# Second MoE on one Trainium2 core: fourteen layer-one products in a run, then the layer-two products of the quad before

## The chip, the cores and the metric

The kernel runs on one core of a Trainium2 chip. The metric is the device time of one execution in microseconds (us), taken as the median of several executions. PE is the matrix engine, DVE, ACT and POOL are the vector, scalar and GpSimd engines, and SP is the engine whose queue issues the transfers here.

## The reference, cut to what matters

The program computes an attention, a dense two-layer network, and a second mixture of experts. Only the last part is touched. It is dense: every expert sees every token.

```python
for e in range(8):                      # N = 2304 tokens, D = 512, F = 1024
    h = np.maximum(x @ w1[e], 0.0)      # layer one: 2304x512 @ 512x1024
    ye = h @ w2[e]                      # layer two: 2304x1024 @ 1024x512
    out += P[:, e:e + 1] * ye           # P: Sinkhorn-balanced gate, 2304x8
```

## The kernel before, in words

Every float32 product is made of three matmuls on rounded halves of the operands (`mm3`, lines 126 to 128: high by high, high by low, low by high). In the second MoE each layer's block product is done by seven products instead of eight (a Strassen-like scheme with sums t1 to t4 of the blocks). A *product* of either layer is six matmuls of 384 columns.

The tokens lie in three blocks of 768. Block one is handled by an earlier stage (layer one from the tile `w1a`, layer two with 512 columns in `values`). Blocks two and three are handled in *quads*: quad m covers 512 columns of one expert's hidden layer, that is two pairs of seven layer-one products, so fourteen; m runs from 16 to 47, sixteen quads a block. Quads 31 and 47, the last of each block, use plain products in layer two (`PLAIN`).

`step(m, s)`, s from 0 to 13, sets the order by hand, for all engines (instructions are issued in the order of the code). A step has one layer-one product s of quad m (`g_product`: weights `w1o`, moving operand `xb..` or `xt..`) and one layer-two product s of quad m-1 (`y_product`: weights `w2o`, moving operand `rb..` or `rt..`). So PE alternates: six matmuls of layer one, six of layer two, and so on.

Layer one of a pair: its seven products (0 to 6, in the order of `GP`) go to three PSUM banks. Products 0, 2, 4 and 5 accumulate in v1 one after the other, product 1 goes to v3, 3 and 6 to v2. After products 0, 2 and 4 ACT must copy v1 out (to m1, u2 and u3) before the next product may add to it. `g_evict` joins the parts: after product 1 DVE adds v3 to m1, after product 4 v2 to u3, after product 6 v2 to u2, each into the temporary, and ACT rectifies the sum (line 1575) into the hidden tile R[m, f, h] (f, h: which 256-column half, which 384-token half). After product 5 ACT rectifies v1 itself. m1 and u3 share one buffer, u2 has its own.

Then R is weighted by the gate (`scaled`, line 1449, DVE), the sums t1 to t4 are made in place (`r_sum`, lines 1454 to 1460, DVE), and each of the seven operands is split: ACT rounds it (`r_hi`, line 1468), POOL takes the rest (`r_lo`, line 1473). Layer two accumulates in four PSUM banks; after each product DVE adds the bank to the output accumulator (line 1509).

SP issues the weights: `load_w1` (line 791) eight layer-one products ahead in a ring of eight buffers, `w2_op` (line 1485) one tile of 512 KB every second step in a ring of nine.

The tiles lie in pools on two sides of SBUF: `w2o` and the operands `rb..`, `rt..` in one pool on the left, `xb..`, `xt..` and `w1o` in two neighbouring pools on the right. In the earlier stage `w1a` lies in the right pool for even pairs n and in the left one for odd n (`split_w1`).

Of the kernel before, what the change touches and what calls it, by code (L numbers as in the profile page):

```python
# [7 lines left out]

F32 = mybir.dt.float32
F32R = mybir.dt.float32r  # L10
U32 = mybir.dt.uint32
AF = mybir.ActivationFunctionType
# [6 lines left out]

F64_SMALL = 2.0 ** -15  # L20
F64_LARGE = 122879.984375


def raw(ap):
# [5 lines left out]
def attention_moe_moe2(  # L30
# [12 lines left out]
    nc = tc.nc  # L43
    P = 128
# [21 lines left out]
    HALF = 3 * P  # L66
    NB = NT // (2 * HALF)
    NPF = F2 // (2 * P)
    NP = E * NPF
# [601 lines left out]
    def gate_logits():  # L671
# [35 lines left out]
        ("t4", 3, 0, False, (1, 0)),  # L707
    ]

    YP_LAST = [  # L710
        ("b11", 0, 0, True),
        ("b21", 2, 0, False, (0, 0)),
# [70 lines left out]

    w1q = {}

    def load_w1(j):

        n, p = divmod(j, 7)
        if NP <= n < NB * NP and j not in w1q:
            w = w1q[j] = p3.tile([P, 2, 2, P], F32R, name="w1o", tag="w1o", bufs=8)  # L790
            nc.sync.dma_start(raw(w), d_w1[n % NP][:, GP[p][0]])

# [367 lines left out]
    def new_temp(nm, tag):  # L1160
        temps[nm] = p2.tile([P, HALF], F32, name=nm, tag=tag, bufs=1)
        return temps[nm]
# [226 lines left out]
    for n in range(NP):  # L1389
        if n == 0:  # L1390

            g_product(0, 0)
            nc.scalar.copy(new_temp("m1", "m"), gb[0][:, :HALF])
            g_product(0, 1)
            nc.vector.tensor_add(temps["m1"], gb[1][:, :HALF], temps["m1"])
            gate_sums(NCH - 1)
            g_product(0, 2)
            nc.scalar.copy(new_temp("u2", "u"), gb[0][:, :HALF])
            gate_logits()
            m1.close()  # L1400
            pp = ctx.enter_context(tc.tile_pool(name="pp", bufs=1))
            wps = ExitStack()
            wp = wps.enter_context(tc.tile_pool(name="wpa", bufs=1))
            acc = [wp.tile([P, 2 * HALF // P, DM], F32, name=f"o{e}") for e in range(2)]
            w2r[0] = raw_w2(0)
            hidden[0] = [wp.tile([P, 2, 2 * HALF], F32R, name=f"r{i}", tag=f"r{i}", bufs=2) for i in "hl"]
            rh, rl = [x[:, 0, :HALF] for x in hidden[0]]
            nc.scalar.activation(rh, temps["m1"], AF.Relu)
            nc.vector.scalar_tensor_tensor(rl, temps["m1"], 0.0, raw(rh), op0=ALU.max, op1=ALU.subtract)
            raw_w1(2)  # L1410
            w2r[1] = raw_w2(1)
            sums_w1(1, False)
        elif n == NP - 2:
            place = acc[1].rearrange("p t d -> p (t d)").rearrange("p (k c) -> p k c", c=HALF)
            x_load(NQ - 1, place, [p2.tile([P, 2, HALF], F32, name="xt", tag="Ra", bufs=4) for _ in range(2)])
        elif n == NP - 1:
            p3s.close()
            p3 = ctx.enter_context(tc.tile_pool(name="p3b", bufs=1, side="right"))
            for j in range(8):
                load_w1(7 * NP + j)  # L1420
        for p in range(3 if n == 0 else 0, 7):
            first_step(n, p)
        before = (n, hidden.pop(n), w2s[n])
        slab.pop(n)
# [20 lines left out]
    def scaled(m, f, h):  # L1445

        pb = pbs[m // NQ, m % NQ // PER][:, h * HALF : (h + 1) * HALF]
        r = R[m, f, h]
        nc.vector.tensor_mul(r, r, pb[:, None, :].to_broadcast([P, 2, HALF]))  # L1449

    def r_sum(m, nm):
        r = {(f, h): R[m, f, h] for f in range(2) for h in range(2)}
        if nm == "t1":
            nc.vector.tensor_sub(r[0, 0], r[0, 1], r[0, 0])  # L1454
        elif nm == "t2":
            nc.vector.tensor_sub(r[0, 0], r[1, 1], r[0, 0])
        elif nm == "t3":
            nc.vector.tensor_sub(r[0, 1], r[1, 1], r[0, 1])
        elif nm == "t4":
            nc.vector.tensor_sub(r[1, 0], r[1, 0], r[0, 0])  # L1460
# [14 lines left out]
    def r_op(m, nm):  # L1475
        r_hi(m, nm)
        if (m, nm) != (total - 1, "b21"):
            r_lo(m, nm, nc.gpsimd)

    def w2_op(m, i):  # L1480
        if m in PLAIN and i > 3:
            return
        o = (0, 2, 1, 3)[i] if m in PLAIN else YP[i][1]
        w = w2q[m, o] = wp.tile([P, 2, 2, 2 * P], F32R, name="w2o", tag="w2o", bufs=9)
        nc.sync.dma_start(raw(w), d_w2[m % NQ][:, o])

    def y_product(m, s):

        i, dt = divmod(s, 2)
        b, op, bk, first, *dsts = (YP_LAST if m in PLAIN else YP)[i]  # L1490
        if m < total - 1:
            bk %= 2
        ps = yb[2 * bk + dt]
        w, x = w2q[m, op], rop[m, b]
        ws = slice(dt * P, (dt + 1) * P)
        for a in range(2):
            mm3(
                ps[:, :HALF], (w[:, a, 0, ws], w[:, a, 1, ws]), (x[:, 0, a], x[:, 1, a]), first and a == 0, a == 1,
                skip_group_check=True,
            )  # L1500
        for dst in dsts:
            key = (m, dst, dt)
            if m % NQ == 0 and key not in touched:
                touched.add(key)
                if dt == 0:
                    acc[dst] = wp.tile([P, 2, HALF], F32, name=f"a{dst[0]}{dst[1]}", tag=f"a{dst[0]}{dst[1]}", bufs=1)
                nc.scalar.copy(acc[dst][:, dt], ps[:, :HALF])
            else:
                nc.vector.tensor_add(acc[dst][:, dt], ps[:, :HALF], acc[dst][:, dt])  # L1509
# [34 lines left out]
    def last_quad():  # L1544
# [16 lines left out]
        for second in range(2):  # L1561
            turn_out(NB - 1, (1, 1), second, yb[second], True)

    def step(m, s):

        nonlocal wp
        if m < total:
            pair, p = divmod(s, 7)

            def rectify(src, f, h):  # L1570
                if pair == 0:
                    R[m, f, h] = (p3 if m % 2 else p2).tile(
                        [P, 2, HALF], F32, name=f"R{f}{h}", tag="Rb" if m % 2 else "Ra", bufs=4
                    )
                nc.scalar.activation(R[m, f, h][:, pair], src, AF.Relu)  # L1575

            g_product(2 * m + pair, p)
            load_w1(7 * (2 * m + pair) + p + 8)
        old = NQ <= m - 1 < total
        if s in EARLY_OPS and m < total:  # L1580
            scaled(m, *EARLY_OPS[s][1:])
        elif s in LATE_OPS and old and m < total:
            if s == 0:
                scaled(m - 1, 0, 1)
            if m - 1 not in PLAIN:
                r_sum(m - 1, LATE_OPS[s])
        if m < total:
            g_evict(p, rectify)
        if s in EARLY_OPS and m < total:
            r_op(m, EARLY_OPS[s][0])  # L1590
        elif s in LATE_SPLITS and old and m < total:
            if m - 1 not in PLAIN:
                r_op(m - 1, LATE_SPLITS[s])
            elif s == 2:
                r_op(m - 1, "t3")
        if old:
            if m - 1 not in PLAIN:
                y_product(m - 1, s)
            else:
                for x in (s,) if s < 12 else (2 * s - 12, 2 * s - 11):  # L1600
                    y_product(m - 1, x)
        if m < total:
            x_switch(m, s)
            if m > NQ:
                if s % 2:
                    w2_op(m, s // 2)
            elif s < 6:
                values(before, (s,))
            elif s == 6:
                wps.close()  # L1610
                wp = ctx.enter_context(tc.tile_pool(name="wpb", bufs=1))
            elif s % 2:
                for i in range(4) if s == 7 else (s // 2,):
                    w2_op(m, i)
            if s == 4 and m % PER == PER - 1 and m + 1 < total:
                load_pb((m + 1) // NQ, (m + 1) % NQ // PER)
        for d in range(2):
            blk, q = divmod(m - d, NQ)
            if q == 0 and blk > 1:
                for dst, at in WHOLE:  # L1620
                    for x in range(2):
                        if at + x == s + 14 * d:
                            turn_out(blk - 1, dst, x, yb[x] if dst == (1, 0) else None)

    load_pb(1, 0)
    store_w2(NP - 1, w2s[NP - 1])
    for m in range(NQ, total):
        for s in range(STEPS):
            if s == 0 and (m + 1) % NQ == 0 and m + 1 < total:
                place = wp.tile([P, 8, HALF], F32, name="q")  # L1630
                x_load(m, place, [wp.tile([P, 2, HALF], F32, name=f"xt{i}") for i in range(2)])
            if (m, s) == (NQ, 7):
                acc = {}
                yb = [y_bank(f"y{i}") for i in range(4)]
            step(m, s)
# [29 lines left out]
```

## Time and profile before

| | us |
|---|---|
| median of 3 runs | 2055.83 (2054.61 to 2056.07) |
| the profiled execution | 2057.16, span 2055.4 |
| PE busy | 2017.4, 98% |
| DVE busy | 1440.3, 70% |
| POOL busy | 1069.4, 52% |
| ACT busy | 986.0, 48% |

The profile is that of one execution. The span runs from its first to its last instruction. A PE row's length is a latency: matmuls overlap, so the spacing of starts tells the rate, not the length.

### The profile page before, as it was taken

To read this page: it belongs to the slowest core of one execution; us is meant where nothing else is said; L and a number is where in the kernel's file an instruction comes from. 1 tells how busy PE (TensorE), PEld (TensorE's weight loads), DVE (VectorE), ACT (ScalarE), POOL (GpSimd) and SP (SyncE) were. 2 spreads that over 40 slices of the span, in tenths; PEclk is the share of its full clock that TensorE was granted. 3 is DMA by queue.
4 is the path that set the end of the run, shared out by engine and by line. 5 is a ranking of instruction groups with operands and counts; after the bars stand their busy time and mean duration, and the time that the engine had idled before them with its cause. 6 is when DMAs were issued, how large, how long until landed. Compare 5 with 4: busy or idle time off the path is not lost.

```text
span 2055.4 us, 31706 instructions
## 1 busy us (share of the span) xinstructions
PE 2017.4 (98%) x10821; PEld 1843.2 (90%) x10821; DVE 1440.3 (70%) x2572; ACT 986.0 (48%) x2006; POOL 1069.4 (52%) x821
## 2 busy tenths in 40 slices
PE   7989999999999999999999999999999999999999
PEld 5767777777888899999989999999999999999998
DVE  7987776565457877777785766776676577667765
ACT  7666665454354454444444434443444444444443
POOL 4224344431168788887884444554455454445442
PEclk9999999999999999999999999999999999999999
DMA  7877777337658878878889778787786877777883
GB/s 203 285 205 243 223 232 203 121 135 262 218 191 327 305 298 324 321 288 308 317 298 336 266 264 257 254 256 260 258 276 213 269 259 258 256 255 240 268 260 103
DMA packets 296416, 519.68 MB, mean 253 GB/s; under 512 B 91056, under 2 KB 137792, under 8 KB 292160
## 3 DMA queue, kind: packets, MB, share of 16 engines
q1 hardware_dynamic: 296256, 517.65, 75.1%
q8 instruction: 87, 1.43, 0.3%
q14 instruction: 73, 0.60, 0.1%
HBM read 356.53 MB, written 161.03 MB: 252 GB/s over the span
## 4 chain that ended last, share of the span: by engine, by line
PE 83%; DVE 6%; ACT 2%; DMA 2%; issue 1%; POOL 1%; SPq 0%; ACTq 0%; DVEq 0%; POOLq 0%
PE y L127 11%; PE y L126 11%; PE y L128 11%; PE g L126 11%; PE g L127 10%; PE g L128 10%; PE s L126 2%; PE s L128 2%; PE s L127 2%; PE acc L127 2%; PE acc L128 2%; PE acc L126 2%; PE h L126 1%; PE h L128 1%; PE h L127 1%
## 5 line engine op out<-in xcount | busy, mean ns | idle before, releaser
L1473 POOL TENSOR_TENSOR rb<-R,rb 128x768 fp32r<-128x768 f32 x95 | 213.9, 2252 | 345.7 <-ACT rb L1468 321.9
L1509 DVE TENSOR_TENSOR a<-y,a 128x384 f32<-128x384 f32 x420 | 232.7, 554 | 192.4 <-PE y L128 192.4
L1473 POOL TENSOR_TENSOR rt<-R,rt 128x768 fp32r<-128x768 f32 x121 | 230.2, 1915 | 138.8 <-ACT rt L1468 59.5
L118 POOL TENSOR_TENSOR w2a<-r,w2a 128x1024 fp32r<-128x1024 f32 x64 | 153.8, 2403 | 67.6 <-ACT w2a L117 67.6
L126 PE MATMUL g<-xt,w1o 128*128 128x384 f32 x512 | 173.7, 339 | 1.8 <-ACT u L1187 1.0
L128 PE MATMUL g<-xt,w1o 128*128 128x384 f32 x512 | 172.6, 337 | 0.0
L127 PE MATMUL g<-xt,w1o 128*128 128x384 f32 x512 | 172.3, 337 | 0.0
L126 PE MATMUL y<-rt,w2o 128*128 128x384 f32 x496 | 168.1, 339 | 0.0
L127 PE MATMUL y<-rt,w2o 128*128 128x384 f32 x496 | 167.9, 339 | 0.0
L128 PE MATMUL y<-rt,w2o 128*128 128x384 f32 x496 | 167.4, 337 | 0.0
L1468 ACT ACTIVATE rt<-R 128x768 fp32r<-128x768 f32 x122 | 102.7, 842 | 134.7 <-DVE R L1454 84.0
L128 PE MATMUL y<-w2a,rl 128*128 128x512 f32 x384 | 150.1, 391 | 0.0
L127 PE MATMUL y<-w2a,rh 128*128 128x512 f32 x384 | 149.6, 390 | 0.2 <-POOL w2a L118 0.2
L126 PE MATMUL y<-w2a,rh 128*128 128x512 f32 x384 | 149.4, 389 | 0.0
L1449 DVE TENSOR_TENSOR R<-R,pb 128x768 f32<-128x768 f32 x128 | 138.5, 1083 | 5.4 <-ACT R L1575 3.9
L126 PE MATMUL y<-rb,w2o 128*128 128x384 f32 x408 | 138.3, 339 | 0.6 <-DVE a L1509 0.6
L127 PE MATMUL y<-rb,w2o 128*128 128x384 f32 x408 | 138.2, 339 | 0.0
L128 PE MATMUL y<-rb,w2o 128*128 128x384 f32 x408 | 137.6, 337 | 0.0
L126 PE MATMUL g<-xb,w1o 128*128 128x384 f32 x384 | 129.9, 338 | 0.0
L128 PE MATMUL g<-xb,w1o 128*128 128x384 f32 x384 | 129.5, 337 | 0.0
L127 PE MATMUL g<-xb,w1o 128*128 128x384 f32 x384 | 129.3, 337 | 0.0
L1575 ACT ACTIVATE R<-u 128x384 f32<-128x384 f32 x128 | 67.3, 526 | 127.6 <-DVE u L1195 86.4
(331 smaller groups left out, 5847.2 us busy)
## 6 DMA issues: line engine op xcount, KB each, us to landing
w1o<-d_w SPq DMA_DIRECT2D x448, 256.0 KB, 3.1
w2o<-d_w SPq DMA_DIRECT2D x218, 512.0 KB, 4.0
d_w<-w1a SPq DMA_DIRECT2D x32, 1792.0 KB, 11.7
d_w<-w2a SPq DMA_DIRECT2D x30, 1536.0 KB, 7.8
r<-in_moe_w_dram SPq DMA_DIRECT2D x64, 512.0 KB, 4.2
u<-in_moe_w_in_dram SPq DMA_DIRECT2D x16, 512.0 KB, 5.0
u<-in_moe_w_out_dram SPq DMA_DIRECT2D x16, 512.0 KB, 5.8
d_in<-a SPq DMA_DIRECT2D x16, 512.0 KB, 2.9
```

What stands on the lines that cost most here:

```text
L118: (eng or nc.gpsimd).tensor_sub(lo, src, raw(hi))
L126: nc.tensor.matmul(ps, lhsT=lh, rhs=rh, start=first, stop=False, **kw)
L127: nc.tensor.matmul(ps, lhsT=lh, rhs=rl, start=False, stop=False, **kw)
L128: nc.tensor.matmul(ps, lhsT=ll, rhs=rh, start=False, stop=last, **kw)
L1449: nc.vector.tensor_mul(r, r, pb[:, None, :].to_broadcast([P, 2, HALF]))
L1468: nc.scalar.activation(x[:, 0], R[m, f, h], AF.Copy)
L1473: eng.tensor_sub(x[:, 1], R[m, f, h], raw(x[:, 0]))
L1509: nc.vector.tensor_add(acc[dst][:, dt], ps[:, :HALF], acc[dst][:, dt])
L1575: nc.scalar.activation(R[m, f, h][:, pair], src, AF.Relu)
```

## The change

For quads 18 to 30 and 34 to 46 (`in_runs`) `run_quad` takes the place of the fourteen calls of `step`. All layer-one products of quad m come in one run, and then all fourteen halves of the seven layer-two products of quad m-1, in the order `Y_RUN`. Product 14 of the run is the first layer-one product of the quad that follows. Four PSUM banks rotate over the pairs (`rbank`). The sum and its rectification, DVE add and ACT Relu before, become one custom DVE instruction that adds and clamps between 0 and the largest float32. The weights, sums and splits of R are put at given places of the run and of the layer-two part (`LATE_RUN`, `ENTRY_RUN` for the first quad of a series, `SCALE_RUN`, `OWN_RUN`). `load_w1` follows a list in the new order (`w1_order`), eight ahead as before; `w2_op` loads the tiles in the order `Y_RUN`. The number of matmuls, their shapes and the bytes moved stay the same.

```diff
+    Y_RUN = [YP[i] for i in (0, 1, 4, 2, 5, 3, 6)]
+    def in_runs(m):
+        return NQ <= m < NB * NQ - 1 and 2 <= m % NQ < NQ - 1
...
+    RUN_STEPS = [1, 2, 3, 4, 7, 5, 6, 8, 9, 10, 11, 14, 12, 13]
+    LATE_RUN = {5: ("t2", "+t4"), 8: ("t4",)}
+    ENTRY_RUN = {1: ("*01", "+t1", "t1"), 4: ("+t3", "t3"), 6: ("+t2", "t2"), 9: ("+t4", "t4")}
+    SCALE_RUN = {14: ("*00",), 13: ("*11",)}
+    OWN_RUN = {
+        0: ("*10",), 1: ("b11",), 2: ("*01",), 4: ("b21",), 6: ("+t1",), 8: ("t1", "+t3"), 10: ("t3",),
+        12: ("b22", "+t2"),
+    }
+    def run_ops(m, ops):     # "*" scaled, "+" r_sum, else r_op (split)
...
+    def run_product(m, s):
...
+        v1, v3, v2 = [rbank[i] for i in ((0, 1, 2), (3, 1, 0), (2, 1, 3))[(j - rfirst[0]) % 3]]
...
+        load_w1(w1_at[14 * m + s] + 8)
...
+        def joined(a, nm, f, h):
+            nc.vector._custom_dve(TENSOR_ADD_SAT, out=own(f, h), in0=a, in1=temps[nm], s0=F32_LARGEST, s1=0.0)
+        if p == 0:
+            nc.scalar.copy(new_temp("m1", "m"), v1)
+        elif p == 1:
+            joined(v3, "m1", 0, 0)
+        elif p == 2:
+            nc.scalar.copy(new_temp("u2", "u"), v1)
+        elif p == 4:
+            nc.scalar.copy(new_temp("u3", "m"), v1)
+            joined(v2, "u3", 1, 1)
+        elif p == 5:
+            nc.scalar.activation(own(1, 0), v1, AF.Relu)
+        elif p == 6:
+            joined(v2, "u2", 0, 1)
...
+    def run_quad(m):
+        entry, leave = not in_runs(m - 1), not in_runs(m + 1)
+        if entry:
...
+            run_product(m, 0)
+        for s in RUN_STEPS:
+            if s < 14 or not leave:
+                run_product(m, s)
+            run_ops(m - 1, (ENTRY_RUN if entry else LATE_RUN).get(s, ()))
+            run_ops(m, SCALE_RUN.get(s, ()))
...
+        for s in range(STEPS):
+            y_product(m - 1, s, Y_RUN)
+            run_ops(m, OWN_RUN.get(s, ()))
+            if s % 2:
+                w2_op(m, s // 2)
...
     for m in range(NQ, total):
+        if in_runs(m):
+            run_quad(m)
+            continue
```

In `step`, the operations of quad m-1 that `run_quad` has done already are skipped for s below 4 (`left`).

## Rows read from the trace of the kernel before

**Rows 1.** The page: busy time by engine, and the granted clock in 40 slices.
```profile
PE 2017.4 (98%) x10821; PEld 1843.2 (90%) x10821; DVE 1440.3 (70%) x2572; ACT 986.0 (48%) x2006; POOL 1069.4 (52%) x821
...
PEclk9999999999999999999999999999999999999999
```
**Rows 2.** Windows, quads 18 to 30 and 34 to 46: length, busy per engine, clock, DMA.
```profile
1137.45:1521.47 384.02, 384.02 (x2185) 384.02 (x2185) 270.73 (x363) 160.15 (x274) 186.75 (x92) 1.00 0.78 256
1617.44:2001.46 384.02, 384.02 (x2185) 384.02 (x2185) 270.73 (x363) 159.69 (x274) 186.91 (x92) 1.00 0.78 256
```
**Rows 3.** Timeline of PE, quad 35: start, length, line, out<-in; every second product's first matmul.
```profile
1646.98 0.34 PE L126 MATMUL g<-xb,w1o 128*128 128x384 f32 x1
...
1649.09 0.34 PE L126 MATMUL g<-xb,w1o 128*128 128x384 f32 x1
...
1651.20 0.34 PE L126 MATMUL g<-xt,w1o 128*128 128x384 f32 x1
```
**Rows 4.** Timeline of PE, layer-two run after the last quad: two products, twelve matmuls apart.
```profile
2035.36 0.33 PE L126 MATMUL y<-rb,w2o 128*128 128x384 f32 x1
...
2037.44 0.33 PE L126 MATMUL y<-rt,w2o 128*128 128x384 f32 x1
```
**Rows 5.** Timeline of PE, block one, even pair: a run of twelve layer-one matmuls.
```profile
927.18 0.34 PE L126 MATMUL g<-xb,w1a 128*128 128x384 f32 x1
...
927.72 0.33 PE L126 MATMUL g<-xb,w1a 128*128 128x384 f32 x1
...
929.28 0.39 PE L126 MATMUL y<-w2a,rh 128*128 128x512 f32 x1
```
**Rows 6.** The same of the next, odd pair.
```profile
942.70 0.34 PE L126 MATMUL g<-xb,w1a 128*128 128x384 f32 x1
...
944.82 0.39 PE L126 MATMUL y<-w2a,rh 128*128 128x512 f32 x1
```
**Rows 7.** Timeline where PE waited for an ACT copy of its bank, quad 16.
```profile
1104.10 0.34 PE L128 MATMUL g<-xt,w1o 128*128 128x384 f32 x1
...
1104.48 0.48 ACT L1187 COPY u<-g 128x384 f32<-128x384 f32 x1
...
1105.01 0.44 PE L126 MATMUL g<-xt,w1o 128*128 128x384 f32 x1 [0.57 <-ACT u L1187]
...
1105.29 0.34 PE L127 MATMUL g<-xt,w1o 128*128 128x384 f32 x1
```
**Rows 8.** Groups by line, 1570 to 2020 us: busy us, mean ns | idle before.
```profile
L1473 POOL TENSOR_TENSOR rt<-R,rt 128x768 fp32r<-128x768 f32 x60 | 113.8, 1908 | 71.1 <-ACT rt L1468 31.7 <-issue 25.6 <-DVE R L1460 13.8
L1509 DVE TENSOR_TENSOR a<-y,a 128x384 f32<-128x384 f32 x201 | 111.4, 554 | 94.3 <-PE y L128 94.3
...
L1449 DVE TENSOR_TENSOR R<-R,pb 128x768 f32<-128x768 f32 x60 | 63.6, 1061 | 2.3 <-ACT R L1575 1.5
...
L1468 ACT ACTIVATE rt<-R 128x768 fp32r<-128x768 f32 x60 | 50.5, 841 | 65.5 <-DVE R L1454 41.4 <-DVE R L1458 24.1
...
L1454 DVE TENSOR_TENSOR R<-R,R 128x768 f32<-128x768 f32 x15 | 34.9, 2327 | 1.6
...
L1187 ACT COPY u<-g 128x384 f32<-128x384 f32 x30 | 14.4, 479 | 54.2 <-PE g L128 54.2
L1460 DVE TENSOR_TENSOR R<-R,R 128x768 f32<-128x768 f32 x15 | 14.2, 948 | 0.0
```
**Rows 9.** Timelines of ACT, POOL and DVE where quad 34 begins (1617.44).
```profile
1617.61 0.83 ACT L1468 ACTIVATE rb<-R 128x768 fp32r<-128x768 f32 x1
...
1621.26 0.85 ACT L1468 ACTIVATE rt<-R 128x768 fp32r<-128x768 f32 x1 [2.08 <-DVE R L1454]
...
1618.80 2.43 DVE L1454 TENSOR_TENSOR R<-R,R 128x768 f32<-128x768 f32 x1
...
1618.52 1.89 POOL L1473 TENSOR_TENSOR rb<-R,rb 128x768 fp32r<-128x768 f32 x1 [0.66 <-ACT rb L1468]
```
**Rows 10.** The page's DMA issues: layer-one weights, KB each, us to landing.
```profile
w1o<-d_w SPq DMA_DIRECT2D x448, 256.0 KB, 3.1
```

More of the change, by code (lines that the diff above doesn't have):

```diff
@@ L5 @@
 from concourse import mybir
+from concourse.dve_ops import TENSOR_ADD_SAT
 from concourse.masks import make_identity
@@ L21 @@
 F64_LARGE = 122879.984375
+F32_LARGEST = 3.4028234663852886e38
 def raw(ap):
@@ L784, in attention_moe_moe2, with load_w1 @@
     w1q = {}
-    def load_w1(j):
-        n, p = divmod(j, 7)
-        if NP <= n < NB * NP and j not in w1q:
+    def in_runs(m):
+        return NQ <= m < NB * NQ - 1 and 2 <= m % NQ < NQ - 1
+    w1_order = []
+    for m in range(NQ, NB * NQ):
+        late = []
+        for p in range(14):
+            if in_runs(m) and p in (5, 6, 12, 13) and (p < 7 or in_runs(m + 1)):
+                late.append(14 * m + p)
+                continue
+            if (m, p) in [(m, 7)] and in_runs(m):
+                w1_order += [14 * m + 7] + late
+                late = []
+            elif p == 0 and in_runs(m) and in_runs(m - 1):
+                continue
+            else:
+                w1_order.append(14 * m + p)
+        if late:
+            w1_order += [14 * m + 14] + late
+    w1_at = {j: i for i, j in enumerate(w1_order)}
+    def load_w1(i):
+        if i < len(w1_order):
+            j = w1_order[i]
+            n, p = divmod(j, 7)
             w = w1q[j] = p3.tile([P, 2, 2, P], F32R, name="w1o", tag="w1o", bufs=8)
@@ L1419, in attention_moe_moe2 @@
             for j in range(8):
-                load_w1(7 * NP + j)
+                load_w1(j)
         for p in range(3 if n == 0 else 0, 7):
@@ L1482, in w2_op, with y_product @@
             return
-        o = (0, 2, 1, 3)[i] if m in PLAIN else YP[i][1]
+        o = (0, 2, 1, 3)[i] if m in PLAIN else (Y_RUN if in_runs(m + 1) else YP)[i][1]
         w = w2q[m, o] = wp.tile([P, 2, 2, 2 * P], F32R, name="w2o", tag="w2o", bufs=9)
         nc.sync.dma_start(raw(w), d_w2[m % NQ][:, o])
-    def y_product(m, s):
+    def y_product(m, s, order=None):
         i, dt = divmod(s, 2)
-        b, op, bk, first, *dsts = (YP_LAST if m in PLAIN else YP)[i]
+        b, op, bk, first, *dsts = (order or (YP_LAST if m in PLAIN else YP))[i]
         if m < total - 1:
@@ L1562, in last_quad @@
             turn_out(NB - 1, (1, 1), second, yb[second], True)
+    RUN_STEPS = [1, 2, 3, 4, 7, 5, 6, 8, 9, 10, 11, 14, 12, 13]
[6 more added lines that the diff above has]
+    }
+    rbank = []
+    def run_ops(m, ops):
+        for o in ops:
+            if o[0] == "*":
+                scaled(m, int(o[1]), int(o[2]))
+            elif o[0] == "+":
+                r_sum(m, o[1:])
+            else:
+                r_op(m, o)
@@ new lines, in run_product, with own @@
+    def run_product(m, s):
+        j, p = divmod(14 * (m - NQ) + s, 7)
+        o, b, bk = GP[p]
+        pair = j % 2
+        quad = NQ + j // 2
+        v1, v3, v2 = [rbank[i] for i in ((0, 1, 2), (3, 1, 0), (2, 1, 3))[(j - rfirst[0]) % 3]]
+        w, x = w1q.pop(14 * m + s), xop[b]
+        for k in range(2):
+            mm3(
+                (v1, v3, v2)[bk][:, :HALF], (w[:, k, 0], w[:, k, 1]), (x[:, 0, k], x[:, 1, k]),
+                p in (0, 1, 3) and k == 0, k == 1, skip_group_check=True,
+            )
+        load_w1(w1_at[14 * m + s] + 8)
+        v1, v3, v2 = [x[:, :HALF] for x in (v1, v3, v2)]
+        def own(f, h):
+            if pair == 0:
+                R[quad, f, h] = (p3 if quad % 2 else p2).tile(
+                    [P, 2, HALF], F32, name=f"R{f}{h}", tag="Rb" if quad % 2 else "Ra", bufs=4
+                )
+            return R[quad, f, h][:, pair]
+        def joined(a, nm, f, h):
[13 more added lines that the diff above has]
+            joined(v2, "u2", 0, 1)
@@ new lines, in attention_moe_moe2 @@
+    rfirst = [0]
+    def run_quad(m):
+        entry, leave = not in_runs(m - 1), not in_runs(m + 1)
+        if entry:
+            rfirst[0] = 2 * (m - NQ)
+            a = [ps_at.tile([P, 512], F32, name=f"rb{i}", tag="at") for i in range(3)]
+            rbank[:] = [a[1], a[0], ps_mm.tile([P, 512], F32, name="rb3", tag="mm"), a[2]]
+            run_product(m, 0)
[4 more added lines that the diff above has]
+            run_ops(m, SCALE_RUN.get(s, ()))
+            if s == 4 and m % PER == PER - 1:
+                load_pb((m + 1) // NQ, (m + 1) % NQ // PER)
+        for s in range(STEPS):
[3 more added lines that the diff above has]
+                w2_op(m, s // 2)
+        if leave:
+            gcount[0] = 3
@@ L1577, in step @@
             g_product(2 * m + pair, p)
-            load_w1(7 * (2 * m + pair) + p + 8)
+            load_w1(w1_at[14 * m + s] + 8)
         old = NQ <= m - 1 < total
+        left = in_runs(m - 1)
         if s in EARLY_OPS and m < total:
             scaled(m, *EARLY_OPS[s][1:])
-        elif s in LATE_OPS and old and m < total:
+        elif s in LATE_OPS and old and m < total and not (left and s < 4):
             if s == 0:
@@ L1590, in step @@
             r_op(m, EARLY_OPS[s][0])
-        elif s in LATE_SPLITS and old and m < total:
+        elif s in LATE_SPLITS and old and m < total and not (left and s < 4):
             if m - 1 not in PLAIN:
@@ L1627, in attention_moe_moe2 @@
     for m in range(NQ, total):
+        if in_runs(m):
+            run_quad(m)
+            continue
         for s in range(STEPS):
```

## The prediction, made before the changed kernel ran

> **What bounds the kernel now.** The page comes first: PE is busy for 98% of the span and its clock is granted at the full level (2.4 GHz) in all 40 slices [rows 1]. The stretch that the change touches is 26 quads, and the windows over them say more: 13 quads take 384.02 us, 29.54 each, twice, with PE busy for every bit of it, the clock at 1.00, DVE at 270.73 of 384.02 and ACT and POOL below half [rows 2]. No wait of PE stands in either stretch. So nothing can be gained there by taking a wait away; only the spacing of the matmuls can get shorter, and whatever wait is added is paid in full.
>
> The spacing is where the reader has to look at starts, not lengths. A step of twelve matmuls, six of layer one and six of layer two, takes 2.11 us (1646.98 to 1649.09 to 1651.20), so 175.8 ns a matmul [rows 3]. 384 columns at 2.4 GHz would be 160. In the layer-two products after the last quad, where nothing alternates, twelve matmuls of the same shape take 2.08 us (2035.36 to 2037.44), 173.3 each [rows 4]. In block one twelve layer-one matmuls come in a run between matmuls of 512 columns. In an even pair, with weights and moving operand both in the right pools, the first three take 0.54 us and the nine after them 1.56 us, 173.3 each [rows 5]. In an odd pair, with weights in the left pool and the operand in the right one, all twelve take 2.12 us, 176.7 each [rows 6]. I read this as a cost of going back and forth between two places of SBUF: nothing in a run within one side, some 3.4 ns a matmul where each matmul's two operands lie on different sides, and something in between where products of two sides alternate. That place is the reason, and not something else that differs, is my inference; that runs go at 173.3 is in the rows.
>
> **What the runs bring.** A changed quad has 168 matmuls: 168 x 0.1733 = 29.12 us against 29.54, so 0.42 less. Two changes of side remain in each. Today a pair of steps (24 matmuls, four changes) takes 4.22 us where 24 x 0.1733 is 4.16, so 0.015 a change; after the change that opens the even run the first three matmuls lose 0.02 [rows 5]. I take 0.025 for each and 0.05 a quad: 0.37 x 26 = 9.6 us less. Bounds: no cost of the changes at all gives 10.9; from below, a run that goes on at today's 175.8 gives 0. I take the near end because both kinds of run are in the trace with these widths, and `w1o` lies in the same pool side as the even `w1a`.
>
> **What the run asks of the copies.** Product 4 adds to the bank that product 2 left, and 5 to that of 4, and ACT must have copied it. Where PE waited for such a copy, the last matmul of a product starts at 1104.10, the copy runs from 1104.48 for 0.48, and PE goes on at 1105.01: 0.91 us from start to start [rows 7]. The matmul after such a wait is slow too, 0.28 to the next instead of 0.17, so 0.11 on top. With one product between, PE gets there after 7 x 0.1733 = 1.21 us, 0.30 later than the copy needs. `RUN_STEPS` puts a product between each such pair (7 between 4 and 5, 14 between 11 and 12), so in 24 quads I count no wait here, as long as ACT stands free when the product ends. It does: in a run ACT has six copies, two rectifications and the splits of t2 and t4 (0.84 each [rows 8]), and these two come after product 5, with three products before the next copy that PE needs.
>
> **The layer-two part.** There DVE has 14 additions to the accumulators at 0.55 (about 0.47 apart when it runs through), two weightings and three sums [rows 8]. A bank is used again four products later. Weightings and sums are short alone and long against POOL: 0.95 for L1460, 2.33 for L1454, of the same shape; 2.43 when it starts at 1618.80 in the middle of POOL's 1618.52 + 1.89 [rows 8, 9]. I lay the queue out from the end of the run (0). `+t3` stands behind the ninth addition, at 10.1 us; POOL splits t1 from 9.8 to 11.7; so `+t3` ends at 12.5, the tenth addition at 13.0, and the last half of t4, which needs that bank, is due at 13.5. That is 0.4 to 0.5 in hand, the least of all banks. DVE then ends 1.6 late and catches up in the next run, where it has six joins.
>
> **The edits that cost nothing.** The one-step join has no row. Its nearest is the PSUM addition of L1509, 0.55; from both sides, half of that gains nothing, because DVE is not what PE waits for, and twice that (1.1) still ends 0.2 before product 6 needs the bank (it has 2.08 us after product 4; copy and hand-over take 0.72) and adds 0.5 to each entry below, 1.1 in all. I take 0.55. Six ACT instructions a quad go away, and ACT was below half busy. Of the queues: SP issues one load of 256 KB per product in a run, 252 GB/s, against 256 GB/s over the stretch now [rows 2], and eight ahead is 8.3 us where landing takes 3.1 [rows 10]; layer-two tiles are issued every second product of the other part, a whole quad ahead. I count nothing; without that cover each late load would be a wait of PE.
>
> **Where waits come in.** The first quad of a series (18 and 34) still has t1 to t4 of the quad before to make, in the run itself. ACT works in order: it stood 2.08 us before the split of t1, waiting for DVE [rows 9]. `ENTRY_RUN` puts that split behind product 1 and ahead of the copy u2. At quad 34: the quad starts its run at 1617.44, product 1 ends at 1619.53, its join at 1620.2. The last split of quad 33 on POOL starts at 1618.52, after ACT's 1617.61 + 0.83, and ends at 1620.4 [rows 9]; the weighting waits for it and ends at 1621.3, `+t1` at 1622.2, the split on ACT at 1623.05, the copy at 1623.5. Product 4 is due at 1621.6 and starts at 1623.55: 1.94 lost, and 0.11 for the slow start. The same happens in small at product 9: `+t2` waits for POOL's half of t3, ACT's split of t2 ends at 1631.3, u2 after it at 1631.8, and product 11 is due at 1630.94: 0.9 and 0.1. Together 3.05 an entry; without any meeting with POOL it is 1.85 (the first wait alone), so 1.85 to 3.05 and I take 3.05, since POOL's splits are where I need them.
>
> The last quad of a series (30 and 46) has no product 14, so 12 follows 11 at once and waits for the copy: 0.91 - 0.17 + 0.11 = 0.84.
>
> **Sum.** -9.6 + 2 x 3.05 + 2 x 0.84 = -1.8 us. The profiled execution took 2057.16 (2055.4 of it span), 1.33 above the median of 2055.83; the sum is made against its rows, and taken off the median gives 2054.0.
>
> **Rivals.**
> - *The entries cost little.* If changes of side cost nothing and an entry has only its first wait in its short form: -10.9 + 3.7 + 1.7 = -5.5, 2050.3. For it: the second wait hangs on one meeting of DVE and POOL. Against it: both lie in the code's order.
> - *The slack in the layer-two part is used up.* One mechanism: `+t3` meets POOL's split of t1 later or longer than laid out, the tenth addition ends over 0.4 us late, and the second half of t4 waits in every quad. It decides from there on; 0.3 late and 0.11 slow start in 24 quads is 9.8, so -1.8 + 9.8 = +8.0, 2063.8. For it: DVE has 1.6 us of arrears by then and its sums were 2.33 on average [rows 8]. Against it: all terms are from rows, and POOL is half idle.
> - *The order of the products changes no spacing.* Then only the added waits are left: +7.8, 2063.6. For it: `w1o` in a run has never been seen; operands near each other might not be what sets 173.3. Against it: 173.3 in both kinds of run, 175.8 between them [rows 3 to 5]. The Trainium skill speaks for this one: "TensorE: Matmul & The Clock Gate", section "Back-to-back issue gap", makes the gap between matmuls a matter of the columns, the weight load and the clock, and knows no price of where operands lie. By it the runs would bring nothing; the same shape at 173.3 and 176.7 [rows 5, 6] disagrees with it.
> - *It doesn't do what it says:* that the runs don't come out in the code's order has nothing for it, since ACT's rows keep that order; no chance of its own.
>
> **Chances.** A measurement of this kernel tells 0.2%, 4.1 us, from no change. Forecast (2051.7 to 2057): 0.48, all within 0.2%. The entries cost little: 0.27, faster. Slack used up: 0.15, of which a quarter is small enough to be no change. No spacing changed: 0.10, slower. So faster 0.27, same 0.52, slower 0.21. The range runs from 2048.5, a little past the cheap entries, to 2063, into both slow cases, and leaves out some 0.2.
>
> **What would show it.** Right: a middle quad takes 29.15 to 29.2 us, PE starts in a run 173 ns apart, waits of PE <- ACT u once or twice in quads 18 and 34 and once in 30 and 46, the join at about 0.55. Wrong: a wait of PE <- DVE a in every quad (second rival), quads still at 29.54 between waits (third), or any wait <- DMA `w1o`, which I hold for excluded.

## The result, and the profile after

The changed kernel takes 2084.04 us (median of four runs, 2080.88 to 2086.5) against 2055.76: ratio 1.0138, interval 1.0119 to 1.0156. It is 28.3 us slower, 21.0 above the upper end of the forecast range. The profiled execution has a span of 2080.0 against 2055.4, so 24.6 more.

The page of the changed kernel, busy time by engine, answers to [rows 1]; its DMA row for the layer-one weights to [rows 10].
```profile
PE 2014.5 (97%) x10821; PEld 1836.8 (88%) x10821; DVE 1433.0 (69%) x2572; ACT 911.7 (44%) x1850; POOL 1059.1 (51%) x821
...
w1o<-d_w SPq DMA_DIRECT2D x448, 256.0 KB, 3.5
```
PE does the same 10821 matmuls in 2.9 us less busy time, in a span that is 24.6 longer. So PE waits, which it hardly did before. The windows over the two series, quads 18 to 30 and 34 to 46, put a place to it; the columns are those of [rows 2].
```profile
1135.03:1532.85 397.82, 384.48 (x2186) 382.10 (x2186) 271.38 (x367) 125.73 (x200) 185.96 (x94) 0.99 0.78 250
1628.76:2025.62 396.86, 383.20 (x2186) 380.50 (x2185) 272.39 (x367) 125.65 (x200) 185.83 (x94) 1.00 0.77 249
```
Each took 384.02 before, with PE busy throughout. Now they are 13.80 and 12.84 longer, 26.6 together, and PE is idle for 13.3 and 13.7 of them. (The rest of the program is 2.0 shorter. Ahead of quad 18, where the two kernels are alike, it is 2.4, and there the granted clock differs: in the windows from 15 to 26 us it is 0.69 before and 0.84 after, from 125 to 131 us 0.72 and 1.00. So this is not from the change.) DVE and POOL have the work they had, ACT 34 us less a series. The waits of PE in the runs name the releaser: us in total, times, longest.
```profile
PE rb L128 <- DMA w1o<-d_w: 21.4, 12, 2.5
PE rb L128 <- ACT u L1641: 4.5, 3, 1.9
PE rb L128 <- ACT u L1643: 1.1, 2, 0.6
```
The last two rows are waits that the prediction counted: three at the entries, where it had four, and two at the leaves. The first is the one that it held for excluded. There are twelve of them in 26 quads: the odd quads from 19 to 29 and from 35 to 45, one each. The windows of quad 19 and of the run of quad 20 show what differs: the run of 19, a stretch inside it, the layer-two part of 19, the run of 20.
```profile
1168.95:1186.32 17.37, 14.86 (x85) 14.57 (x85) 6.63 (x9) 5.33 (x10) 7.12 (x4) 1.00 0.80 191
1176.95:1180.95 4.00, 4.00 (x25) 4.00 (x25) 0.62 (x2) 1.30 (x3) 3.48 (x2) 1.00 0.97 86
1186.32:1200.91 14.59, 14.59 (x86) 14.59 (x86) 14.05 (x20) 4.12 (x5) 6.98 (x4) 1.00 0.89 304
1200.91:1215.50 14.59, 14.59 (x86) 14.59 (x86) 6.62 (x9) 5.33 (x10) 7.11 (x4) 1.00 0.69 204
```
A run without the wait takes 14.59, 84 matmuls at 173.7 ns, and the layer-two part the same: the quad is 29.17 or 29.18, where 29.54 - 0.37 = 29.17 was forecast. The run of quad 19 takes 2.78 more. The last two columns of the second row are what the reader should look at: for 4 us the DMA engines are busy for 0.97 of the time and move only 86 GB/s. Of the 506 packets in this stretch 436 have 512 bytes. What they carry stands in SP's timeline of that run and in the list of its DMA issues (count, KB each, median us to landing).
```profile
1170.21 3.44 SPq L818 DMA_DIRECT2D w1o<-d_w  x4
1173.74 0.39 SPq L1461 DMA_DIRECT2D pb<-d_p  x1
1174.37 12.46 SPq L818 DMA_DIRECT2D w1o<-d_w  x10
```
```profile
w1o<-d_w SPq DMA_DIRECT2D x14, 256.0 KB, 6.0
...
pb<-d_p SPq DMA_DIRECT2D x1, 384.0 KB, 9.6
```
`pb` is the broadcast table of gate weights for the next expert, 384 KB in 768 packets of 512 bytes, loaded in every odd quad behind product 4 of the run (`load_pb` in `run_quad`). It lands after 9.6 us. The first `w1o` load behind it is issued at 1174.37, and its product, the 13th of the run, starts late:
```profile
1184.14 0.41 PE L128 MATMUL rb<-xt,w1o 128*128 128x384 f32 x1 [2.51 <-DMA w1o<-d_w]
1184.39 0.34 PE L129 MATMUL rb<-xt,w1o 128*128 128x384 f32 x1
```
The matmul before it started at 1181.29, so its weights were due at 1181.46, 7.1 us after the issue of their load; PE went on 9.8 after the issue. The matmul after the wait is 0.25 away instead of 0.17.

In three places more follows a wait: quads 23 and 35, and quad 18 after its wait for ACT, have ten or eleven matmuls 0.32 apart. The window over that stretch of quad 18 shows the granted clock at 0.50, the lower level of 1.2 GHz; PE had stood for 1.87 us before 1141.22 and had run without a gap from there.
```profile
1142.80:1145.20 2.40, 2.40 (x9) 2.40 (x8) 1.42 (x2) 0.85 (x2) 0.00 (x0) 0.50 0.37 109
```
Each stretch costs some 1.6 us. The ten other odd quads wait 1.35 to 2.5 us and keep the full level, and so does quad 34 after 1.87; what decides it, the rows don't show.

Intervals between matmuls above 173.3 ns, added up, give the account of the change in us. (The loads' row can be read from the quads too: from start to start the twelve odd ones take 30.77 to 33.07 us, the even ones between them 29.17.)

| term | forecast | measured |
|---|---|---|
| runs, 26 quads | -9.6 | -9.6 (26 x 0.37) |
| entries, quads 18 and 34 | +6.1 | +6.9 (3.70 and 3.15) |
| leaves, quads 30 and 46 | +1.7 | +1.7 (0.84 each) |
| loads behind `pb`, 12 odd quads | 0 | +27.5 |
| sum | -1.8 | +26.5 (windows: +26.6) |

### The profile page after: what moved, and what is told of

Read it like the earlier page. It is cut to its first block, busy times and chain, and to the rows that moved or that the text cites. A ratio compares the mean times of both kernels' runs of the same rounds, so it can differ in the third digit from the quotient of the medians.

```text
span 2080.0 us, 31581 instructions
## 1 busy us (share of the span) xinstructions
PE 2014.5 (97%) x10821; PEld 1836.8 (88%) x10821; DVE 1433.0 (69%) x2572; ACT 911.7 (44%) x1850; POOL 1059.1 (51%) x821
## 4 chain that ended last, share of the span: by engine, by line
PE 76%; DMA 7%; DVE 7%; ACT 3%; issue 1%; POOL 1%; SPq 0%; ACTq 0%; DVEq 0%; POOLq 0%
PE y L129 11%; PE y L130 11%; PE y L128 11%; DMA w1o<-d_w 5%; PE rb L128 5%; PE rb L130 5%; PE rb L129 5%; PE g L128 4%; PE g L130 4%; PE g L129 4%; PE s L128 2%; PE s L129 2%; PE s L130 2%; PE acc L129 2%; PE acc L130 2%; PE acc L128 1%
## 5 line engine op out<-in xcount | busy, mean ns | idle before, releaser
L1500 POOL TENSOR_TENSOR rt<-R,rt 128x768 fp32r<-128x768 f32 x121 | 225.3, 1873 | 255.2 <-ACT rt L1495 237.7
L1536 DVE TENSOR_TENSOR a<-y,a 128x384 f32<-128x384 f32 x420 | 218.3, 549 | 48.9 <-PE y L130 46.0
L1634 DVE CUSTOM_DVE_ANT_0 R<-rb,u 128x384 f32<-128x384 f32 x104 | 58.0, 557 | 221.8 <-ACT u L1643 135.2
L128 PE MATMUL rb<-xt,w1o 128*128 128x384 f32 x416 | 141.0, 339 | 27.0 <-DMA w1o<-d_w 21.4
L1476 DVE TENSOR_TENSOR R<-R,pb 128x768 f32<-128x768 f32 x128 | 160.3, 1253 | 3.0 <-ACT R L1686 2.6
L129 PE MATMUL rb<-xt,w1o 128*128 128x384 f32 x416 | 139.5, 335 | 0.0
L130 PE MATMUL rb<-xt,w1o 128*128 128x384 f32 x416 | 139.4, 335 | 0.0
L1495 ACT ACTIVATE rb<-R 128x768 fp32r<-128x768 f32 x96 | 80.8, 842 | 111.8 <-PE y L130 105.5
L1344 ACT ACTIVATE rh<-g 128x384 fp32r<-128x384 f32 x127 | 62.3, 491 | 136.3 <-DVE g L1216 53.5
L1345 DVE SCALAR_TENSOR_TENSOR rl<-g,rh 128x384 fp32r<-128x384 f32 x127 | 70.7, 557 | 69.9 <-ACT rh L1344 69.8
```

The costliest lines, as they stand in the source:

```text
L128: nc.tensor.matmul(ps, lhsT=lh, rhs=rh, start=first, stop=False, **kw)
L129: nc.tensor.matmul(ps, lhsT=lh, rhs=rl, start=False, stop=False, **kw)
L130: nc.tensor.matmul(ps, lhsT=ll, rhs=rh, start=False, stop=last, **kw)
L1344: nc.scalar.activation(rh, src, AF.Relu)
L1345: nc.vector.scalar_tensor_tensor(rl, src, 0.0, raw(rh), op0=ALU.max, op1=ALU.subtract)
L1495: nc.scalar.activation(x[:, 0], R[m, f, h], AF.Copy)
```

## The experiments

The theory after the trace: the transfer of `pb` in front of the run's loads is the whole loss, since a run leaves a load 7.1 us from its issue to its product, where the alternating products left 15.6. Rivals: SP itself is held, or a run at this rate of loads is too much for the DMA engines in any order. The later runs ask what set the spacing of 175.8.

**The load of `pb` behind the run.**
```
-            if s == 4 and m % PER == PER - 1:
-                load_pb((m + 1) // NQ, (m + 1) % NQ // PER)
 ...
+        if m % PER == PER - 1:
+            load_pb((m + 1) // NQ, (m + 1) % NQ // PER)
         for s in range(STEPS):
```


> The changed kernel with one move: the load of the gate weights (tile pb, every second quad) is issued behind the run, at the head of the layer-two part, instead of behind product 4 of the run. Theory (the pb transfer holds the DMA engines for some 6 us, and in a run the layer-one weights are only 7 us ahead): the 12 waits of PE for w1o (21.4 us) and the slow matmuls after them go, 27 us together, so 2057 us, and only the entry and leave waits stay. Rival one (a run simply asks more of the DMA engines than they give, wherever pb lies): waits for w1o stay, 2075 or more. Rival two (SP is held at pb's issue, waiting for its buffer): the place behind the run would cure that too, so this run doesn't tell it from the theory; the next one does.

Measured: 2055.5 (2053.7 to 2057.34), ratio to before 0.9998 (0.9989 to 1.0007). The waits of PE lose the one row and keep the others:
```profile
PE rb L128 <- ACT u L1641: 4.5, 3, 1.9
PE rb L128 <- ACT u L1643: 1.1, 2, 0.6
```
The DMA issues from 1134 to 1500 us say that `pb` itself has become no faster; it only stands in front of the layer-two part, which uses no `w1o`.
```profile
w1o<-d_w SPq DMA_DIRECT2D x178, 256.0 KB, 3.1
...
pb<-d_p SPq DMA_DIRECT2D x6, 384.0 KB, 9.0
```
So 28.5 us, the whole loss, hung on the place of one transfer. No run waits for a load, so the rate of loads in a run is not the trouble.

**The same place, the same bytes, long packets.** The table is stored with an expert's weights side by side, and a partition gets them in one packet of 3 KB instead of six of 512 bytes.
```
-    d_p = dram.tile([NTT * E, P], F32, name="d_p")
+    d_p = dram.tile([E, NTT, P], F32, name="d_p")
 ...
-        nc.sync.dma_start(d_p[:P], pt[:, 0])
-        nc.sync.dma_start(d_p[P:], pt[:over, 1])
+        for t in range(NTT):
+            r = t * E % P
+            nc.sync.dma_start(d_p[:, t], pt[r : r + E, t * E // P])
 ...
-        src = d_p.rearrange("(t e) p -> e t p", e=E)[e, blk * nt : (blk + 1) * nt]
+        src = d_p[e, blk * nt : (blk + 1) * nt].rearrange("t p -> (t p)")
 ...
```


> The changed kernel with pb loaded at the same place, but from a copy of the gate laid out by expert, so that each partition gets one packet of 3 KB instead of six of 512 B; bytes, queue, waits and place are the same. Theory (the number of short packets is what holds the DMA engines): the pb load lands in under 5 us instead of 8.8, the w1o loads behind it in under 6 instead of 9.6, and the waits go: 2057 to 2062 us. Rival (its bytes or its 128-fold broadcast from one row are the price, or SP's wait for the buffer): landing and waits as they are, 2080 to 2087.

Measured: 2052.99 (2052.28 to 2054.79), ratio 0.999 (0.9981 to 0.9999), a little below the expected 2057 to 2062. The expected landing times can't be compared, since this run's profile has no landings. `pb` is issued where it was, at 1172.82 with SP held for 0.37, and no run waits. In its stretch of quad 19 the engines are as full and move four times as much:
```profile
1176.00:1180.00 4.00, 4.00 (x25) 4.00 (x24) 0.63 (x2) 1.30 (x3) 3.50 (x2) 1.00 1.00 344
```
The pages of the changed kernel and of this one have the same bytes and 10,128 packets less:
```profile
DMA packets 296416, 519.68 MB, mean 250 GB/s; under 512 B 91056, under 2 KB 137792, under 8 KB 292160
```
```profile
DMA packets 286288, 519.68 MB, mean 253 GB/s; under 512 B 91168, under 2 KB 125616, under 8 KB 282032
```
So neither the bytes nor the place as such was at fault, but the way the table was cut. Nor was SP: in quad 19 of the changed kernel it is held too, but at a load issued 3.1 us after the one that PE waited for.
```profile
1177.49 2.41 SPq L818 DMA_DIRECT2D w1o<-d_w  x1
```
Whether the count of packets, their length or the scattered source makes the price, this run doesn't separate. The Trainium skill, "DMA: Bandwidth & Descriptors", section "Specifications", gives 512 bytes as the length from which a transfer goes at line rate; here packets of just that length, 768 of them in a broadcast, kept the engines busy at 86 GB/s. Here that length alone didn't give it.

**The join alone.** The kernel before with nothing but the one-step join in quads 18 to 30 and 34 to 46.
```
-            nc.vector.tensor_add(c, v3, temps["m1"])
-            rectify(c, 0, 0)
+            if joined:
+                joined(v3, "m1", 0, 0)
+            else: ...
```


> The kernel before with one part of the change alone: in quads 18 to 30 and 34 to 46 sum and rectification in one custom DVE instruction, the order of the products as before. My prediction's term (nothing: PE doesn't wait for DVE or ACT there): 2055.8, within 2 us; quads at 29.54. Rival (a custom DVE instruction costs something of its own, or a shorter ACT queue gives something): off by more than 4 us either way.

Measured: 2058.71 (2057.43 to 2062.42), ratio 1.0018 (1.0008 to 1.0027): about 3 us slower, which I had not expected. All its quads but the first of each series take 29.70 instead of 29.54, with the loss at one place. DVE around the start of quad 36, two of its instructions 10 us apart, and PE there:
```profile
1676.83 2.52 DVE L1459 TENSOR_TENSOR R<-R,pb 128x768 f32<-128x768 f32 x1
...
1687.23 0.54 DVE L1519 TENSOR_TENSOR a<-y,a 128x384 f32<-128x384 f32 x1
```
```profile
1687.58 0.34 PE L129 MATMUL g<-xt,w1o 128*128 128x384 f32 x1
1687.83 0.44 PE L127 MATMUL y<-rt,w2o 128*128 128x384 f32 x1
1688.11 0.34 PE L128 MATMUL y<-rt,w2o 128*128 128x384 f32 x1
```
I read it so: the join comes out earlier than add and rectify did, the weighting L1459 falls into POOL's split of 1676.69 to 1678.53 and takes 2.52, where the next takes 0.94 (0.95 and 1.37 in the kernel before), and DVE is late from there: the addition at 1687.23 ends at 1687.77, and the matmul that reuses its bank starts at 1687.83, 0.25 after its forerunner instead of 0.17, with 0.28 to the next. The wait of 0.07 stands in no row of the waits. The join itself takes 0.54, as forecast, and in the old order it still wasn't free.

**Entry and leave without waits.** On the first experiment: each split at the entry one step later than its sum, and the first half product of layer two in the place of the missing product 14 at the leave.
```
-    ENTRY_RUN = {1: ("*01", "+t1", "t1"), 4: ("+t3", "t3"), 6: ("+t2", "t2"), 9: ("+t4", "t4")}
+    ENTRY_RUN = {1: ("*01", "+t1"), 4: ("t1", "+t3"), 6: ("t3", "+t2"), 9: ("t2", "+t4"), 11: ("t4",)}
 ...
+            else:
+                y_product(m - 1, 0, Y_RUN)
 ...
-            y_product(m - 1, s, Y_RUN)
+            if s or not leave:
+                y_product(m - 1, s, Y_RUN)
```


> The first of these kernels with two more edits: in the first quad of a series each split follows one place later, behind the copy that PE needs; in the last quad of a series the first half product of layer two stands between products 11 and 12. By the terms of the prediction the entries lose nothing instead of 3.4 (as measured) and the leaves nothing instead of 0.84: 8.5 us less than the kernel with the later load alone, so 2048 to 2050 us, 0.3% faster than before: the 9.6 us of the runs, bare. If the runs brought nothing it would be 2056.

Measured: 2046.55 (2044.99 to 2047.23), ratio 0.9955 (0.9942 to 0.9967). No wait of PE is left in the runs; a window of 378 us in the first series is busy to the end:
```profile
1135.00:1513.00 378.00, 378.00 (x2179) 378.00 (x2178) 268.50 (x364) 125.06 (x200) 189.03 (x93) 1.00 0.80 263
```
This is the bare worth of the runs, 9.2 us where 9.6 was forecast.

**The same entry and leave on the long packets.**

> The changed kernel with pb in long packets at its old place, and with the entry and leave edits; nothing else. The two repairs so far are of separate waits, so their effects should add: the kernel with long packets alone took 2053.0, the two edits were worth 8.5 by the rows and 9.0 as measured beside the later load, so 2044 to 2045 us. If the long packets and the edits work on the same time, 2047 or more.

Measured: 2045.44 (2043.36 to 2046.58), ratio 0.9947 (0.9934 to 0.9961). Nothing to choose between the two mends.

**Distance of the operands.** The prediction took 175.8 and 176.7 for the price of two places in SBUF. In the kernel before, an unused tile moves the weights of the odd pairs in block one up by 32 KB, from byte 92864 of a partition to 125632, nearer to the operand.
```
         w2r[0] = raw_w2(0)
+        wp.tile([P, 8, 2, 2 * P], F32R, name="w2a", tag="w2a", bufs=2)
```


> The kernel before with one tile moved: in block one the weights w1a of the odd pairs lie 32 KB higher in the left pool (125632 instead of 92864 bytes into the partition), nearer to the operands xb and xt (183264 and up), and w2a 39 KB lower; the instructions and their order are unchanged. Theory of the prediction, sharpened (the distance between a matmul's two operands sets the spacing, not the pool or the parity of the pair): products b11, b21, t1 of odd pairs, now 43 to 75 KB apart instead of 76 to 107, go at 173 to 174 ns instead of 176.7, those farther apart may stay. 16 pairs of 42 matmuls at 3.3 ns are 2.2 us at the most, so 2053.5 to 2056. Rival (something else that differs between even and odd pairs): odd pairs stay at 176.7 throughout, 2055.8.

Measured: 2055.86, ratio 1.0002 (0.9993 to 1.0011). Twelve matmuls of an odd pair take 2.12, as in [rows 6]:
```profile
942.79 0.34 PE L126 MATMUL g<-xb,w1a 128*128 128x384 f32 x1
...
944.91 0.39 PE L126 MATMUL y<-w2a,rh 128*128 128x512 f32 x1
```
The same tile on the fifth kernel:

> The first of these three with the tile of the second moved as well. If distance sets the spacing in block one, up to 2.2 us less than the first of these three: 2042 to 2044 us; if not, equal to it.

Measured: 2046.2, ratio 0.9953 (0.994 to 0.9965), the fifth kernel's within the intervals. So distance, as far as this move tells, is not the price.

**Thirty-two bytes.** What differs as well: every tile of the right pools starts 32 bytes past a multiple of 64, those of the left pools on one (right 183264 and 213984, left 27328 and 64192, from the built program). In the kernel before, an unused tile of 32 bytes under the right pools puts all on multiples of 64. No order changes.
```
+    ctx.enter_context(tc.tile_pool(name="pad", bufs=1, side="right")).tile([P, 8], F32, name="pad")
     m1 = ExitStack()
```


> The kernel before with one unused tile of 32 bytes at the bottom of the right pools: every tile there lies 32 bytes lower, at a multiple of 64 bytes like those of the left pools, where before they lay 32 past one. Instructions, order and distances are as before. Neither distance nor pool explains block one (the slab moved up kept 176.7); what even pairs, the last layer-two products and the runs share is that weights and operand lie alike against 64 bytes. Theory (a change of that offset from one read to the next costs, not the alternation of layers): quads go from 29.54 to 29.15 us without any run, odd pairs from 176.7 to 173.4 ns: 30 quads at 0.39 and 16 odd pairs at 0.14 are 14 us, so 2041 to 2043 us. Rival (going back and forth between the two sides costs, wherever in 64 bytes they lie): 2055.5, quads at 29.54.

Measured: 2044.89 (2042.23 to 2045.83), ratio 0.9949 (0.9936 to 0.9963). The alternating products of quad 35, which answer to [rows 3], now stand 2.08 apart for twelve, 173.3 ns each, and the 13 quads of [rows 2] take 378.56 in both series, 29.12 each:
```profile
1637.52 0.33 PE L127 MATMUL g<-xb,w1o 128*128 128x384 f32 x1
...
1639.60 0.33 PE L127 MATMUL g<-xb,w1o 128*128 128x384 f32 x1
...
1641.68 0.33 PE L127 MATMUL g<-xt,w1o 128*128 128x384 f32 x1
```
```profile
1134.90:1513.46 378.56, 378.56 (x2185) 378.56 (x2185) 270.96 (x363) 159.73 (x274) 185.78 (x92) 1.00 0.79 260
1608.40:1986.96 378.56, 378.56 (x2185) 378.56 (x2185) 270.98 (x363) 159.61 (x274) 185.77 (x92) 1.00 0.80 259
```
One unused tile gives 10.8 us, about all that the runs were to bring, with the products in their old order and on their old sides. PE is busy throughout in both kernels, so what became shorter is the spacing itself, and what the runs avoided in the quads is a price that hangs on where the right pools start.

That multiples of 64 are the rule is not shown. A shift of 64 bytes, which would leave the place against 64 as it is, was not run, and block one speaks against it: I had expected 173.4 ns for its odd pairs and 2041 to 2043 us. With everything on multiples of 64 the first twelve matmuls of a pair there take 2.11, 175.5 each, in even and odd pairs alike, where it was 174.4 and 176.7 before:
```profile
924.43 0.33 PE L127 MATMUL g<-xb,w1a 128*128 128x384 f32 x1
...
926.54 0.39 PE L127 MATMUL y<-w2a,rh 128*128 128x512 f32 x1
```

**Both.** The fifth kernel with the 32 bytes:

> The kernel with runs, long packets and the entry and leave edits (2045.4), with the same 32 bytes. If the offset is what costs, the runs have nothing left to save: this gains only in the odd pairs (2.2 us), in the quads outside the runs and in the earlier stages, and ends beside the kernel before with 32 bytes, within 2 us of it. If sides cost, it stays at 2045.

Measured: 2043.54 (2041.8 to 2043.92), ratio 0.994 (0.9928 to 0.9953), the lowest median of all runs and, as forecast for this case, within 2 us of the eighth. Its middle quads take 29.12 like those of the eighth.

**Only the weights moved.** The kernel before with the 32 bytes under the pool of `w1o` alone: weights on multiples of 64, `xb` and `xt` still 32 past one.
```
+            ctx.enter_context(tc.tile_pool(name="pad", bufs=1, side="right")).tile([P, 8], F32, name="pad")
             for j in range(8):
```


> The kernel before with the 32 bytes under the pool of w1o alone: the layer-one weights lie at multiples of 64 bytes, their moving operands xb and xt still 32 past. If the offset costs within a matmul as in the odd pairs of block one, the layer-one products of the quads go at 176 to 177 ns and a quad takes 29.4 to 29.7 us; if only the pool side matters, 29.54 as before.

Measured: 2046.14, a single run. Quads take 29.21, below all that I expected; layer-one products stand at 173.3, and a little is left in the layer-two product after each change (matmuls at 175 and 179 ns):
```profile
1640.25 0.34 PE L126 MATMUL g<-xb,w1o 128*128 128x384 f32 x1
...
1642.34 0.34 PE L126 MATMUL g<-xb,w1o 128*128 128x384 f32 x1
```
The odd pairs of block one, with the very same pair of offsets, stay at 176.7. So offsets against 64 alone don't tell the price, and which pair of places costs how much isn't settled.

**Old order, 32 bytes, long packets.** The ninth kernel without runs and join:

> The kernel before, products alternating, with the 32 bytes and pb in long packets: all of the best kernel but the runs, the join and what they need. If the runs are worth nothing once the offset is right, it takes what the best kernel takes, 2043 to 2044.5 us (the same run of the two differed by 1.4 us without the packets); if the runs still bring something, 2045 or more.

Measured: 2044.29 (2042.8 to 2045.51), ratio 0.9947 (0.9934 to 0.9961). The ninth kernel's 0.994 (0.9928 to 0.9953) overlaps with it: with the 32 bytes in, 0.8 us is what the runs may add, and it isn't told from nothing.

## Why the prediction was wrong

- *The step that failed* stands under "The edits that cost nothing": "eight ahead is 8.3 us where landing takes 3.1 ... I count nothing". The median of 448 loads stood for each of them. Of what the moved step issues, `load_pb` was left out, though the trace of before had it: `pb` landing after 8.4 us (median of the first series), and the `w1o` load behind it after 7.0 to 9.7. There it was hidden: the one behind `pb` in quad 19 is issued at 1178.79, and its product starts at 1194.43, 15.6 us later (the DMA issues, SP's timeline and PE's).
```profile
pb<-d_p SPq DMA_DIRECT2D x6, 384.0 KB, 8.4
...
1178.79 0.32 SPq L791 DMA_DIRECT2D w1o<-d_w  x1
...
1194.43 0.34 PE L126 MATMUL g<-xb,w1o 128*128 128x384 f32 x1
```
The run cut this cover to 7.1, not 8.3, because a load is issued when the last matmul of its buffer is done. The cost is 27.5 us by the intervals and 28.5 by the first experiment; the second shows that the way the table was cut sets it.

- *Runs*: right in size, 29.17 a quad, 9.2 us by the fourth experiment. The reason given, going between two places of SBUF, was wrong: in the eighth the quads go at 173.3 ns with the same sides in the same order, after a shift of 32 bytes. What the price follows stays open. The prediction had marked the reason as inference, and the number, taken from rows, didn't hang on it.
- *Entries and leaves*: 3.70 and 3.15 for 3.05, 0.84 for 0.84. In quad 18 the second wait didn't come, and a stretch at the lower clock, 1.6 us, took its place; that 3.70 comes near 3.05 is luck.
- *Join*: 0.55 right for the instruction. As an edit by itself, in the old order, it costs 3 us. By the reading above, an earlier weighting met more of POOL's split.
- *Rivals*: "The slack in the layer-two part is used up" had nothing in the trace; no wait on `a` in any quad of the runs. "The order changes no spacing" was wrong for this kernel and holds with the 32 bytes, where a quad takes 29.12 with runs (ninth) and without (eighth). The rule named there, in the Trainium skill's "TensorE: Matmul & The Clock Gate", section "Back-to-back issue gap", has no term for where the operands start; the quads show 173.3 and 175.8 for one shape by 32 bytes alone.
- *The sum without the failed step*, 2054.0, stands within the interval of the first experiment (2055.5, ratio 0.9989 to 1.0007).

## What to carry to other kernels

Ask of each load in a regrouped loop not how long a median landing takes but how long the one behind the largest or most finely cut transfer of its queue takes, and set that against the new time from issue to use. Look for busy DMA engines at low GB/s: here this was a transfer to cut into longer packets. Before matmuls are reordered for their spacing, shift a pool by some bytes: it is a one-line experiment, and here it gave as much as the reordering (10.8 us against 9.2, with intervals that overlap).

## What was not expected of the hardware

- Matmuls of 384 columns in the alternating quads go at 173.3 ns or at 175.8 by a 32-byte shift of the right pools alone; over the kernel that is 10.8 us. The same shift leaves the first twelve of a pair in block one at 175.5.
- A broadcast load of 384 KB in 512-byte packets kept the DMA engines at 0.97 and 86 GB/s over 4 us, and PE could use a load behind it only 9.8 us after its issue. In 3 KB packets the engines moved 344 GB/s in its stretch.
- After three of the fourteen waits of 1.35 to 2.5 us PE was granted the lower clock (0.50) for ten or eleven matmuls.
- A wait of 0.07 us, too short for the list of waits, and the 0.10 of slow start behind it made a quad 29.70 us instead of 29.54.
